# Talking-heads attention with a squared-ReLU feed-forward: reciprocals, copies and tails moved to GpSimd, spread weights made later, and another order of TensorE's units

## The chip, the cores and the metric

The kernel runs on one core of a Trainium2 chip. The metric is the time of one execution on the device in microseconds, as the median of several runs. A lower time is better. Beside the timed runs there is one profiled execution with a hardware trace.

The engines are called by their names or by the short names of the profile: TensorE (PE, and PEld for its weight loads), VectorE (DVE), ScalarE (ACT), GpSimd (POOL) and SyncE (SP). A name with a q behind it (SPq, POOLq) is the engine's queue when it issues a DMA.

## The reference

The inputs are q, k and v of shape (8 batches, 12 heads, 448 positions, 64), two 12 x 12 matrices w_pre and w_post, and the weights of a feed-forward layer, w_in (768 x 2048) and w_out (2048 x 768). All are float32.

```python
scores = scale * np.matmul(q, k.transpose(0, 1, 3, 2))
scores = np.einsum('bhij,hg->bgij', scores, w_pre)      # mixes heads before the softmax
scores = scores - np.max(scores, axis=-1, keepdims=True)
attn = np.exp(scores)
attn = attn / (np.sum(attn, axis=-1, keepdims=True) + 1e-09)
attn = np.einsum('bhij,hg->bgij', attn, w_post)         # mixes heads after it
attn_out = np.matmul(attn, v)
x = attn_out.transpose(0, 2, 1, 3).reshape(B * S, H * D)
h = np.maximum(x @ w_in, 0.0)
out = h * h @ w_out                                     # 3584 x 768, float32
```

## The kernel before, in words

**Pieces of work.** The kernel handles the eight batches one after another, overlapped. For a batch it loads q and k, reorders them by copies from qraw and kraw into qkt (`fn_shf`, "shf", one copy for each of q and k and each of three groups of heads, in batches 1 to 7), transposes them on TensorE, evicts the transposes, and multiplies q by k (`emit_QK`) for tiles of rows. The scores are evicted to `stage` and moved by DMAs on SyncE's queue into `dring`, so that the 12 heads of 10 query rows stand in 120 partitions. Such a set of 10 rows is a chunk, and two chunks are a pair. One matmul group for each pair (`emit_pre`) mixes the heads.

**The softmax.** `after_pre` does the rest for a pair. ScalarE takes the exp out of PSUM into `pring` and sums each row into `sums` (L1215). The reciprocal of the sums goes to `rinv` (`fn_rec`, L1231, VectorE). The division isn't done on the scores but on the weights of the second mixing: `fn_fold` (L1238) multiplies wk2b by `rinv` into `wk2s`, one set of weights for each chunk. The last 64 columns of both chunks use shared weights, so there `fn_tail` (L1249) multiplies the scores themselves by `rinv` into `ptail`. For the first five pairs (`g < 10`) reciprocal, fold and tail are on VectorE. After that the fold is on GpSimd, and the tail goes to VectorE or GpSimd as the planner finds. `emit_post` then mixes the heads with `wk2s` and `ptail`, the result is evicted into `a2t` ("a2ev", L1304), and `emit_AV` multiplies by v. `rinv`, `wk2s`, `pring` and `ptail` are rings of 10 chunks, five pairs: a new pair waits for the users of the pair five before it (`old_users`).

**Feed-forward.** `emit_F1` multiplies by w_in, the ReLU is taken out of PSUM by ScalarE or VectorE (L1458, L1459), VectorE squares (L1468), and `emit_F2` multiplies by w_out. GpSimd issues the output DMAs (L1588), and the loads of q, k, v and the weights.

**The start.** In batch 0 the first chunks go without the moves. VectorE multiplies q by weights (`sc`, L948) and TensorE takes six chunks directly (L1028). Sixteen further chunks take scores from a spread copy of q (L985), and mix heads with `wk1s` (L1006). `wk1s` is made on VectorE (L570) from `wrep3`, which four small DMAs on ScalarE's queue fill (`fn_wspread`, L557). The profile calls this tile wrep too.

**What sets the order.** A planner written in Python (`_Plan`) runs when the kernel is built. Each task has an engine, dependencies, a priority, and for each engine that may do it a pair of times in ns: how long it holds the engine, and when its result is there. TensorE's units are taken from ten streams in the order that the string `ORDER` gives, one character a unit (0 transposes, 1 and c scores, 2, a and b the first mixing in three forms, 3 the second mixing, 4 the multiplication by v, 5 the direct and spread start, 6 to 9 the feed-forward). The other engines take whichever ready task can start earliest, then by priority. A task marked FLEX goes to the engine that would end it first, with `bias` added on VectorE's side. So a changed cost moves nothing by itself but can move tasks between engines and change their order. Each engine then executes its list strictly in the planned order, and semaphores make it wait where the real times are later than the planned. A unit of TensorE that uses the array in another form than the one before it ("quad", "row", "cols", "full") has a change of mode planned at 102 ns. A task marked `two` on VectorE is planned to wait while a `two` task of GpSimd runs.

Of the kernel before, what the change touches and what calls it, by code (L numbers as in the profile page):

```python
# [7 lines left out]
ALU = mybir.AluOpType  # L8
# [20 lines left out]
INF = float("inf")  # L29
STREAM = {"a": 2, "b": 2, "c": 1, **{str(i): i for i in range(10)}}  # L30
ORDER = (
    "00c0010c501551555c55555515555c15555553531c5213a5b5aaa525b030255553aa03250232353c0ab3a03a"
    "c143c244312c673a623bb63762a37763b6ca76173337331c142cb4ba41367673a66727633cc7663227776633"
    "17ac919229393383b002441182383128300240027ac18a3c811c83c3836c3ca67222667733c6631761327722"
    "24442763cc763c36c3761ca002767322276673336621277833811283a8022083003811181318222919133931"
    "39222449c1c933a931393224422443226336c37117c6ca36100a7337321621672237a006336371273422008c"
    "18113811382229392229393181a183338c3c83124222444422363c6c17337a1631603a073c721621673a3736"
    "221673370022442200931933c9c229c8c18a3382218c9c33913a93393114222444228381338c3183c622267a"
    "37c6300c63722176126733373622167220073930019ca393c19c83c182228183c83228a1833c833c4b422244"
    "442236cc63371c76336c62226701077c37362216733722803082218380330913c9c22911922913933c913392"  # L40
    "228c8a3c83383cc4422244442226736373c6cc62276c771c6373621267337812283383382214442293392229"
    "39363368222838338a7367767676733684447667766776677676768798989989899988"
)


# [282 lines left out]
def bass_talking_heads_attention__then__ffn_squared_relu_kernel(  # L328
# [45 lines left out]
    with ExitStack() as es:  # L374
        def sb(name, shape, dtype):
            return es.enter_context(nc.sbuf_tensor(name, list(shape), dtype))
# [34 lines left out]
        nmax = sb("nmax", [128, NPS, 2], DT.float32)  # L411
        test = sb("test", [128, 4], DT.float32)
        flag = sb("flag", [1, 1], DT.int32)
        rinv = sb("rinv", [128, NPS, 1], DT.float32)
        sb("align", [128, 16], DT.uint8)
        w_in_sb = sb("w_in_sb", [128, NFT, FF], DT.bfloat16)
# [42 lines left out]
        def program(safe):  # L459
# [35 lines left out]

            def fn_init(eng, en):
                eng.memset(mask[:, :, :], 1.0)
                eng.memset(wk1r[:, :], 0.0)
                eng.memset(wk1c[:, :, :], 0.0)
                eng.memset(wrep[:, :], 0.0)  # L500
                eng.memset(wk2b[:, :, :], 0.0)
                eng.memset(wk1s[:, :], 0.0)
                eng.memset(wrep3[:, :], 0.0)
                return eng.memset(ident[:, :], 0.0)
# [48 lines left out]
            def fn_wspread(eng, en):  # L553
                for x in range(4):
# [3 lines left out]
                        sem_w3.handle, 16)  # L558
                return None

            t_wspread = plan.add("wspread", ACT, fn_wspread, [t_init], {ACT: (2900.0, 6000.0)},
                                 -1e6, sem_w3, 64)

            def fn_wk1s(eng, en):
# [256 lines left out]
            def emit_T(b):  # L821
                pb = b % 2
                for a in range(3):
                    g = _Group(2)
                    trs = []
                    for i, src in enumerate((qraw, kraw)):
                        o0 = i * S
                        if b == 0:
                            g = _Group(1)
                            o0 = 0  # L830

                        def fn_tr(eng, en, a=a, g=g, i=i, src=src, o0=o0):
                            r_ = None
                            for t in range(0 if b else 2 * NT):
                                o = ((POS[t % NT] if i else t % NT) * 2 + t // NT) * 32
                                for c in range(2):
                                    rows = slice(64 * c, 64 * c + 64)
                                    o_ = ps_bf[rows, g.banks[0], 0:2 * S].rearrange(
                                        "p (u k) -> p u k", u=2)[:, :, o:o + 32]
                                    i_ = src[rows, 2 * a + t // NT, t % NT, :]  # L840
                                    r_ = eng.transpose(o_, i_, ident[rows, rows])
                            for t in range(NT if b else 0):
                                o = o0 + (POS[t] if i else t) * PJ
                                for u in range(2):
                                    rows = slice(64 * u, 64 * u + 64)
                                    i_ = qkt[rows, pb, a, i, :, :].rearrange("p u s -> p (u s)")
                                    r_ = eng.transpose(ps_bf[:, g.banks[u], o:o + PJ],
                                                       i_[:, 2 * D * t:2 * D * (t + 1)],
                                                       ident[rows, rows])
                            return r_  # L850

                        landed = [t_ for t_ in qk_tasks[(b, a)] if t_.name[8:9] == str(i)]
                        if b:
                            def fn_shf(eng, en, a=a, i=i, src=src):
                                return copy(
                                    eng, en,
                                    qkt[:, pb, a, i, :, :].rearrange(
                                        "p u s -> p (u s)").rearrange(
                                        "p (t c d) -> p t c d", c=2, d=D),
                                    src[:, 2 * a:2 * a + 2, :, :].rearrange("p c t d -> p t c d"))  # L860

                            t_shf = add("shf%d_%d_%d" % (b, a, i), FLEX, fn_shf,
                                        landed + [qk_done.get(b - 2)],
                                        {DVE: (400.0, 500.0), POOL: (1500.0, 1620.0)},
                                        b * 1000.0 - 710)
                            t_shf.two = True
                            landed = [t_shf]
                            raw_free[(b, a, i)] = t_shf
                        t_tr = unit(s_T, "tr%d_%d_%d" % (b, a, i), fn_tr, landed + [t_init2],
                                    7 * 32.0 + 20.0 if b else 14 * 32.0 + 33.0,  # L870
                                    "row" if b else "quad", g, 2 * NT if b else 4 * NT)
                        T_of[(b, a, i)] = t_tr
                        raw_free.setdefault((b, a, i), t_tr)
                        trs.append(t_tr)
                        if b:
                            continue
                        for u in range(2):
                            p = 3 * u + a

                            def fn_ev(eng, en, u=u, p=p, g=g, i=i):  # L880
                                return copy(eng, en, qkt[:, 0, p % 3, i, p // 3, :],
                                            ps_bf[:, g.banks[0], u * S:(u + 1) * S])

                            t_ev = add("tev0_%d_%d" % (p, i), FLEX, fn_ev, [t_tr, trev.get((0, p - 3, i))],
                                       {ACT: (447.0, 597.0), DVE: (309.0, 400.0)}, -4e5)
                            g.readers[0].append(t_ev)
                            trev[(0, p, i)] = t_ev
                            if i:
                                trev[(0, p)] = t_ev
                            else:  # L890
                                emit_scale(p)
                                emit_spread(p)
# [252 lines left out]
            def old_users(g):  # L1145
                x = g - g % 2 - NPS
                return [d.get(y) for d in (post_of, fold_of, tail_of) for y in (x, x + 1)]
# [45 lines left out]
            def after_pre(g, t_pre, gr, x):  # L1193
# [34 lines left out]
                p0 = g0 % NPS  # L1228

                def fn_rec(eng, en):  # L1230
                    return eng.reciprocal(rinv[:, p0:p0 + n, :], sums[:, g0:g0 + n, :])  # L1231

                t_rec = add("rec%d_%d" % (b, c), DVE, fn_rec, [exp_of[g0], t_exp] + old_users(g),
                            {DVE: (82.0, 160.0)}, b * 1000.0 - 900 + c)

                def fn_fold(eng, en):
                    i0 = wk2b[:, :, :].rearrange("p a b -> p (a b)").unsqueeze(1)
# [3 lines left out]

                t_fold = add("fold%d_%d" % (b, c), DVE if g < 10 else POOL, fn_fold,
                             [t_rec, t_wk2] + old_users(g),
                             {POOL: (330.0, 370.0), DVE: (200.0, 280.0)},
                             b * 1000.0 - 900 + c)
                t_fold.two = True

                def fn_tail(eng, en):
# [3 lines left out]

                t_tail = add("tail%d_%d" % (b, c), DVE if g < 10 else FLEX, fn_tail,
                             [t_rec, t_exp, exp_of[g0]] + old_users(g),
                             {POOL: (390.0, 430.0), DVE: (210.0, 290.0)},
                             b * 1000.0 - 900 + c)
                t_tail.two = True
                for y in members(g0):
                    fold_of[y] = t_fold
                    tail_of[y] = t_tail  # L1260
# [3 lines left out]
            def emit_post(g0):  # L1264
# [32 lines left out]
                for x in range(n):  # L1297
                    def fn_a2(eng, en, x=x):
# [3 lines left out]
                            "p (o t) -> p o t", t=H5))  # L1302

                    t_a2 = add("a2ev%d_%d" % (g0, x), FLEX, fn_a2, [t_post] + old,  # L1304
                               c_ev(nb * PR), b * 1000.0 - 800 + c0)
                    for g in gs:
                        a2_of[g].append(t_a2)
                    gr.readers[x].append(t_a2)
# [527 lines left out]
```

## Time and profile before

| | |
|---|---|
| median of 3 runs | 539.87 us (537.53 to 541.67) |
| the profiled execution, its time | 539.18 us |
| its span, first to last instruction | 537.4 us |
| mean granted TensorE clock | 0.992 |
| instructions | 22056 |
| bytes moved by DMA | 72.08 MB, mean 134 GB/s |
| DMA issues on GpSimd for outputs, loads of q and k, loads of v | 52, 88, 48 |

The span is shorter than the time by 1.8 us, which lie before the first and after the last instruction. A busy share is the share of the span in which an engine executed. A row of a group names the line, the engine, the operation, the tiles written and read, the shapes and the count. Behind the first bar stand the busy us and the mean ns of one. Behind the second bar stands the idle time just before these instructions and what ended it. In a list of waits the three numbers are total us, times, and longest us. TensorE's busy time counts matmuls from their start to their modelled end, and these overlap, so short gaps between them are not seen.

### The profile page before, as it was taken

The numbers are of one execution on the slowest core, as the hardware profiler recorded it, in microseconds if no ns is written. First come the engines' busy times: TensorE is split into PE (matmuls) and PEld (weight loads), VectorE is DVE, ScalarE is ACT, GpSimd is POOL, SyncE is SP. The second block draws the span as 40 slices with busy tenths as digits, with TensorE's granted clock in tenths as the row PEclk, the third lists the DMA queues.
The fourth block names the chain that finished last, engine by engine and source line by source line (L and its number), as shares of the span: only waits on it lengthen the run. The fifth ranks groups of instructions, "written<-read, shape, count | busy, mean of one in ns | idle before, by whom it ended". The sixth has DMA issues, their size and how long they took to land.

```text
span 537.4 us, 22056 instructions
## 1 busy us (share of the span) xinstructions
PE 512.1 (95%) x8924; PEld 318.9 (59%) x8924; DVE 439.9 (82%) x1187; ACT 454.7 (85%) x1295; POOL 230.9 (43%) x430
## 2 busy tenths in 40 slices
PE   6898999999999999999989998899999999999997
PEld 3345666657765664566546664366645574567964
DVE  6699998899998889978998887987889776977530
ACT  5599999899999899999988897789889998898411
POOL 9513664433572475435653356422923244033000
PEclk9799999999999999999999999999999999999999
DMA  8979999856795589557873589436964566543004
GB/s 175 199 153 156 183 211 182 159 121 133 150 181 124 126 162 166 119 116 153 166 145 73 130 172 180 106 69 141 183 129 98 127 152 131 98 96 73 4 17 107
DMA packets 82519, 72.08 MB, mean 134 GB/s; under 512 B 13502, under 2 KB 79662, under 8 KB 82414
## 3 DMA queue, kind: packets, MB, share of 16 engines
q0 software_dynamic: 36480, 32.58, 38.2%
q1 hardware_dynamic: 45514, 37.83, 29.6%
q8 instruction: 73, 1.20, 0.9%
q10 hardware_dynamic: 420, 0.20, 0.1%
q14 instruction: 32, 0.26, 0.1%
HBM read 45.70 MB, written 11.01 MB: 106 GB/s over the span
## 4 chain that ended last, share of the span: by engine, by line
PE 58%; ACT 20%; DVE 14%; DMA 4%; issue 2%; ACTq 0%; SPq 0%; DVEq 0%
PE ps L1553 23%; PE ps L1425 11%; ACT pring L1215 9%; ACT a2t L486 5%; PE ps L1347 5%; DVE stage L487 4%; PE ps L1285 4%; PE ps L1087 4%; PE ps L1177 4%; ACT stage L486 3%; DVE a2t L487 3%; DMA dring<-stage 2%; PE ps L1399 2%; PE ps L1496 2%; DVE h2t L1468 2%
## 5 line engine op out<-in xcount | busy, mean ns | idle before, releaser
L1215 ACT ACTIVATE pring<-ps 128x448 bf16<-128x448 f32 (+1 forms) x368 | 197.7, 577 | 10.3 <-PE ps L1177 8.0
L1238 POOL TENSOR_TENSOR wk2s<-wk2b,rinv 128x120 bf16<-128x120 bf16 x179 | 76.2, 428 | 192.3 <-DVE rinv L1231 191.7
L1553 PE MATMUL ps<-w_out_sb,h2t 64*128 64x384 bf16 x1664 | 152.0, 323 | 0.3
L1425 PE MATMUL ps<-xt,w_in_sb 64*128 64x448 bf16 (+2 forms) x1344 | 121.8, 322 | 1.4 <-DVE a2t L487 0.8
L486 ACT ACTIVATE a2t<-ps 128x420 bf16<-128x420 f32 x182 | 113.2, 686 | 9.9 <-PE ps L1285 9.2
L487 DVE CAST a2t<-ps 128x420 bf16<-128x420 f32 x178 | 110.6, 648 | 8.8 <-PE ps L1285 7.3
L487 DVE CAST stage<-ps 128x448 bf16<-128x448 f32 (+1 forms) x179 | 107.6, 616 | 11.8 <-PE ps L1087 8.3
L1553 PEld LDWEIGHTS ps<-w_out_sb,h2t 64*128 64x128 bf16 x1664 | 79.0, 94 | 51.4 <-PE ps L1177 2.1
L486 ACT ACTIVATE stage<-ps 128x448 bf16<-128x448 f32 (+1 forms) x181 | 95.0, 568 | 17.1 <-PE ps L1087 16.1
L1215 ACT ACTIVATION_READ_ACCUMULATOR pring<-ps 128x1 f32 (+1 forms) x368 | 89.2, 242 | 0.0
L1425 PEld LDWEIGHTS ps<-xt,w_in_sb 64*128 64x128 bf16 x1344 | 62.1, 94 | 42.0 <-PE ps L1177 2.3
L1588 POOL DMA_DIRECT2D out_dram<-osb x52 | 33.7, 653 | 89.0 <-DVE osb L487 37.5
L1285 PEld LDWEIGHTS ps<-wk2s,pring 60*128 60x128 bf16 x2160 | 52.0, 93 | 30.0 <-issue 3.4
L1285 PE MATMUL ps<-wk2s,pring 60*128 60x60 bf16 x2160 | 60.7, 187 | 4.8 <-DVE rinv L1231 1.5
L1468 DVE TENSOR_TENSOR h2t<-h1t 128x448 bf16<-128x448 bf16 (+2 forms) x176 | 59.6, 367 | 1.4 <-ACT h1t L1458 1.0
L1087 PE MATMUL ps<-qkt 64*128 64x448 bf16 (+1 forms) x360 | 54.1, 356 | 6.6 <-DVE qkt L487 4.2
L1458 ACT ACTIVATE h1t<-ps 128x448 bf16<-128x448 f32 (+2 forms) x98 | 44.1, 470 | 15.4 <-PE ps L1425 13.4
L1249 DVE TENSOR_TENSOR ptail<-pring,rinv 128x128 bf16<-128x128 bf16 x166 | 55.3, 333 | 2.0
L1231 DVE RECIPROCAL rinv<-sums 128x2 f32<-128x2 f32 x184 | 28.9, 157 | 27.2 <-ACT pring L1215 26.6
L1459 DVE TENSOR_SCALAR h1t<-ps 128x448 bf16<-128x448 f32 (+2 forms) x78 | 37.7, 485 | 10.7 <-PE ps L1425 9.6
L1177 PE MATMUL ps<-dring,wk1r 64*64 64x448 bf16 (+1 forms) x550 | 41.1, 362 | 3.4 <-issue 2.1
L1399 PE MATMUL ps<-xt,w_in_sb 128*128 128x220 bf16 (+1 forms) x384 | 42.2, 260 | 0.3 <-ACT a2t L486 0.2
(87 smaller groups left out, 604.9 us busy)
## 6 DMA issues: line engine op xcount, KB each, us to landing
dring<-stage SPq DMA_DIRECT2D x308, 105.0 KB
out_dram<-osb POOLq DMA_DIRECT2D x52, 192.0 KB, 3.9
qraw<-in_q_dram POOLq DMA_DIRECT2D x42, 112.0 KB, 5.3
kraw<-in_k_dram POOLq DMA_DIRECT2D x42, 112.0 KB, 5.0
w_in_sb<-in_moe_w_in_dram POOLq DMA_DIRECT2D x8, 384.0 KB, 8.7
vraw<-in_v_dram POOLq DMA_DIRECT2D x24, 128.0 KB
w_out_sb<-in_moe_w_out_dram POOLq DMA_DIRECT2D x8, 384.0 KB, 11.7
vraw<-in_v_dram POOLq DMA_DIRECT2D x24, 96.0 KB
```

What stands on the lines that cost most here:

```text
L486: return eng.activation(o, i_, AF.Copy)
L487: return eng.tensor_copy(o, i_)
L1087: r_ = eng.matmul(ps[o:o + i_, g.banks[x], 0:S], qkt[r0:r0 + 64, pb, p_ % 3, 0, p_ // 3, i0 + w - i_:i0 + w], qkt[r0:r0 + 64, pb, p_ % 3, ...
L1177: r_ = eng.matmul(ps[64 * y:64 * y + 64, gr.banks[x], 0:S], wk1[64 * x:64 * x + 64 - R0 * x, :], dring[64 * x:64 * x + 64 - R0 * x, (g0 + ...
L1215: return eng.activation(pring[0:r1, pr, 0:S], ps[0:r1, gr.banks[x], 0:S], AF.Exp, accum_out=sums[0:r1, g, :], **bias)
L1238: return eng.tensor_tensor(wk2s[:, p0:p0 + n, :], i0.to_broadcast([128, n, PR]), rinv[:, p0:p0 + n, :].to_broadcast([128, n, PR]), ALU.mult)
L1249: return eng.tensor_tensor(ptail[:, p0 // 2, :, :], pring[:, p0:p0 + n, 0:PJ], rinv[:, p0:p0 + n, :].to_broadcast([128, n, PJ]), ALU.mult)
L1285: r_ = eng.matmul(ps[:, gr.banks[x], o * PR:(o + 1) * PR], p_, w_, start=True, stop=True)
L1399: r_ = eng.matmul(ps[:, g.banks[0], 0:n], w_in_sb[:, ft, t * 128:(t + 1) * 128], xt[:, ft, c0:c1], start=(ft == 0), stop=(ft == NFT - 1))
L1425: r_ = eng.matmul(ps[z * m:(z + 1) * m, g.banks[x], 0:n], w_in_sb[64 * y:64 * y + 64, ft, t:t + m], xt[64 * y:64 * y + 64, ft, c0:c1], sta ...
L1468: return eng.tensor_tensor(h2t[:, t16, o0:o0 + n], h1t[:, s, 0:n], h1t[:, s, 0:n], ALU.mult)
L1553: r_ = eng.matmul(ps[z * m:(z + 1) * m, g.banks[hh], 0:FH], h2t[64 * y:64 * y + 64, t16, col + z * m:col + (z + 1) * m], w_out_sb[64 * y:6 ...
```

## The change

- `fn_rec`: for every pair after the first five the reciprocal is done on GpSimd, as `sums` to the power -1, with a constant tile `minus` as the second operand. One memset for it is added at the start. For the first five pairs it stays on VectorE.
- `fn_shf`: the copy of head pairs may no longer go to VectorE. All are on GpSimd.
- `fn_tail`: VectorE's side gets a bias of 300 ns in the planner's choice, and the costs are changed.
- The fold's cost on GpSimd and the eviction of the second mixing (`a2ev`) get other figures in the planner.
- `t_wspread`: the four small DMAs are planned to hold ScalarE for 3.4 us instead of 2.9, and to have landed 11.6 us after the task's start instead of 6.0. What waits for them is planned later.
- `ORDER` is another string of the same 950 units.

```diff
 ORDER = (
-    "00c0010c501551555c55555515555c15555553531c5213a5b5aaa525b030255553aa03250232353c0ab3a03a"
+    "00c0010c5c05511555555555155555153555522c51225b550c05c1b553325bbb533a5b3a2530a03bb300c3c3"
...
+        minus = sb("minus", [128, 2, 1], DT.float32)
         rinv = sb("rinv", [128, NPS, 1], DT.float32)
...
                 eng.memset(mask[:, :, :], 1.0)
+                eng.memset(minus[:, :, :], -1.0)
...
-            t_wspread = plan.add("wspread", ACT, fn_wspread, [t_init], {ACT: (2900.0, 6000.0)},
+            t_wspread = plan.add("wspread", ACT, fn_wspread, [t_init], {ACT: (3400.0, 11600.0)},
                                  -1e6, sem_w3, 64)
...
-                            t_shf = add("shf%d_%d_%d" % (b, a, i), FLEX, fn_shf,
+                            t_shf = add("shf%d_%d_%d" % (b, a, i), POOL, fn_shf,
                                         landed + [qk_done.get(b - 2)],
-                                        {DVE: (400.0, 500.0), POOL: (1500.0, 1620.0)},
+                                        {POOL: (990.0, 1050.0)},
...
                 def fn_rec(eng, en):
+                    if en == POOL:
+                        return eng.tensor_tensor(rinv[:, p0:p0 + n, :], sums[:, g0:g0 + n, :],
+                                                 minus[:, 0:n, :], ALU.pow)
                     return eng.reciprocal(rinv[:, p0:p0 + n, :], sums[:, g0:g0 + n, :])
 
-                t_rec = add("rec%d_%d" % (b, c), DVE, fn_rec, [exp_of[g0], t_exp] + old_users(g),
-                            {DVE: (82.0, 160.0)}, b * 1000.0 - 900 + c)
+                t_rec = add("rec%d_%d" % (b, c), DVE if g < 10 else POOL, fn_rec,
+                            [exp_of[g0], t_exp] + old_users(g),
+                            {DVE: (82.0, 160.0), POOL: (130.0, 170.0)}, b * 1000.0 - 900 + c)
...
-                             {POOL: (330.0, 370.0), DVE: (200.0, 280.0)},
+                             {POOL: (344.0, 400.0), DVE: (200.0, 280.0)},
...
-                             {POOL: (390.0, 430.0), DVE: (210.0, 290.0)},
+                             {POOL: (350.0, 400.0), DVE: (200.0, 290.0)},
                              b * 1000.0 - 900 + c)
                 t_tail.two = True
+                t_tail.bias = 300.0
...
                     t_a2 = add("a2ev%d_%d" % (g0, x), FLEX, fn_a2, [t_post] + old,
-                               c_ev(nb * PR), b * 1000.0 - 800 + c0)
+                               {ACT: (501.0, 610.0), DVE: (543.0, 632.0)}, b * 1000.0 - 800 + c0)
```

More of the change, by code (lines that the diff above doesn't have):

```diff
@@ L31 @@
 ORDER = (
-    "00c0010c501551555c55555515555c15555553531c5213a5b5aaa525b030255553aa03250232353c0ab3a03a"
[L33 to L42, printed above, removed]
+    "00c0010c5c05511555555555555155553555522c51225b550c05c1b553325bbb533a5b3a2530a03bb300c3c3"
+    "1ac424c4c233a66262772336236b732763b7133763336211444711721aa6662c37733667c323766713a77627"
+    "319c221938293390023812414a8321833430a00270ac8112811c8333811622766231767ca66cc27733336722"
+    "244413267c763c166c37273003176223762267722166738a33812183382200830308ccc811382229c933c933"
+    "19c2244293119ac93339223422444b3a6316337c17136a36100a732c73126126722370063363721272438220"
+    "083318c1181c93a39222939a813c8c3381c381324222444423161a36373137c6a1c6a00733712621673337a6"
+    "12260073372244220093c9ccc93c19228318ca383228c933c933a93c193224442224838113833622816c1733"
+    "722006136a7223763363722176a3367112790000c9c3c91cc92228382238a38a383c381c383cc81324422244"
+    "4422367361c7c6c163700a176333637221762236721178a008333831822290091319a319229339cc39133922"
+    "24418cc833a8c13832244442226716c71631631731733622267a376212673378121833833822244422933933"
+    "922298382238633687a677367633766444877667767686767767676789989999888899"
 )
```

## The prediction

> **What bounds the kernel now.** I read the shares of the page first, then the chain that ended last, then a table of busy time by stage, then the stretches that looked empty.
>
> ```profile
> span 537.4 us, 22056 instructions
> PE 512.1 (95%) x8924; PEld 318.9 (59%) x8924; DVE 439.9 (82%) x1187; ACT 454.7 (85%) x1295; POOL 230.9 (43%) x430
> ...
> PE 58%; ACT 20%; DVE 14%; DMA 4%; issue 2%; ACTq 0%; SPq 0%; DVEq 0%
> ```
>
> TensorE is busy for 95% of the span. Nothing in the change shortens a matmul, so what can be won is what TensorE waits for. That 34% of the chain runs through ScalarE and VectorE says who makes it wait: they empty the eight PSUM banks. The stages (columns: stretch, its length, then busy time of PE, PEld, DVE, ACT and POOL, granted clock, DMA share, GB/s) show where:
>
> ```profile
> 10.00:17.00 7.00, 2.43 (x62) 1.36 (x62) 2.78 (x11) 3.67 (x10) 5.83 (x10) 0.77 1.32 199
> 17.00:25.00 8.00, 8.00 (x60) 3.25 (x58) 5.71 (x19) 4.64 (x11) 3.63 (x5) 0.77 1.33 200
> 25.00:75.00 50.00, 47.69 (x837) 26.96 (x837) 47.37 (x134) 49.87 (x157) 21.39 (x39) 1.00 0.98 174
> 75.00:500.00 425.00, 412.82 (x7405) 258.74 (x7403) 366.17 (x960) 383.94 (x1092) 188.79 (x353) 1.00 0.68 134
> ```
>
> From 10 to 17 us TensorE works 2.43 of 7 us. From 25 to 75 us ScalarE is full and VectorE nearly so. From 75 to 500 us TensorE misses 425 - 412.82 = 12.2 us. The timeline tells what happened at the start:
>
> ```profile
> 11.46 0.63 PE L841 MATMUL ps<-ident,qraw 64*64 64x64 bf16 x28 [0.37 <-DMA qraw<-in_q_dram]
> 14.84 0.35 DVE L570 SCALAR_TENSOR_TENSOR wk1s<-wrep,mask 128x60 bf16<-128x60 f32 x2 [4.19 <-DMA wrep<-in_w_pre_dram]
> 16.12 0.56 PE L1087 MATMUL ps<-qkt 64*128 64x448 bf16 x2 [4.03 <-DVE qkt L487]
> 17.47 0.95 PE L841 MATMUL ps<-ident,kraw 64*64 64x64 bf16 x28
> 22.04 0.36 PE L1087 MATMUL ps<-qkt 64*128 64x448 bf16 x2
> ```
>
> VectorE stood 4.19 us in front of wk1s, an instruction that waits for the spread weights. Behind it in VectorE's queue stood the evictions of the transposes (qkt) that TensorE needed, so TensorE stood 4.03 us. Its clock then fell: the same 28 transposes took 0.63 us before and 0.95 us after.
>
> **The change part by part.** The prices come from the groups by line, shapes apart:
>
> ```profile
> L1231 DVE RECIPROCAL rinv<-sums 128x2 f32<-128x2 f32 x184 | 28.9, 157 | 27.2 <-ACT pring L1215 26.6
> L1249 DVE TENSOR_TENSOR ptail<-pring,rinv 128x128 bf16<-128x128 bf16 x166 | 55.3, 333 | 2.0
> L1249 POOL TENSOR_TENSOR ptail<-pring,rinv 128x128 bf16<-128x128 bf16 x18 | 7.3, 403 | 0.0
> L487 DVE COPY qkt<-kraw 128x896 bf16<-128x896 bf16 x11 | 6.7, 605 | 0.0
> L487 POOL COPY qkt<-qraw 128x896 bf16<-128x896 bf16 x12 | 11.4, 950 | 2.1 <-DMA qraw<-in_q_dram 2.1
> L1238 POOL TENSOR_TENSOR wk2s<-wk2b,rinv 128x120 bf16<-128x120 bf16 x179 | 76.2, 428 | 192.3 <-DVE rinv L1231 191.7
> L517 POOL TENSOR_SCALAR_AFFINE_SELECT mask<-mask 128x10 f32<-128x10 f32 x2 | 0.4, 220 | 0.0
> ```
>
> *Spread weights later.* The planner now expects them 11.6 us after their task starts, which by its own figures (ScalarE free at 1.3 us, initialisation first) is about 1.9 us; so wk1s is due at 13.5 us. VectorE could start it at 14.84, so up to 1.3 us of the wait may stay: the gain is 2.7 to 4.0 us, and I take 3.4. Its only readers, the matmuls of L1006, come after scores that are spread and evicted behind the whole start, so the later place costs nothing. With the stall goes the low clock. From 17 to 25 us TensorE was full at clock 0.77, so at most 8 x 0.23 = 1.8 us, at least nothing if the scaled products of VectorE come last there; I take 0.8. The Trainium skill's page "TensorE: Matmul & The Clock Gate", Part 1, says that an idle window of about 3.4 us puts the clock at half. The trace agrees (4.03 us idle, then 0.95 against 0.63 us); by that rule a rest of 1.3 us would leave the clock whole and the term would be the full 1.8. Start: **-4.2** (-2.7 to -5.8).
>
> *VectorE relieved from 25 to 75 us.* Three tables by stretch, of VectorE's reciprocals, of the tails (VectorE, then GpSimd), and of its copies from qraw and kraw:
>
> ```profile
> 25.00:75.00 50.00, 3.66 (x23) 1.00 0.98 174
> 75.00:500.00 425.00, 25.24 (x161) 1.00 0.68 134
> ...
> 25.00:75.00 50.00, 5.72 (x19) 1.59 (x4) 1.00 0.98 174
> 75.00:500.00 425.00, 49.60 (x147) 5.66 (x14) 1.00 0.68 134
> ...
> 25.00:75.00 50.00, 1.21 (x2) 1.00 0.98 174
> ...
> 25.00:75.00 50.00, 0.61 (x1) 1.00 0.98 174
> ```
>
> The first five pairs keep VectorE for reciprocal and tail. So 18 reciprocals leave (18 x 0.157 = 2.8 us), half of 14 tails (7 x 0.30 = 2.1) and three copies (1.8): 6.7 us. Evictions go to whichever engine is free, so both full engines share it: 3.4 us at most, nothing if the exps alone, which only ScalarE can do, set the pace. TensorE's own idle time there is 2.3 us. I take **-1.7** (0 to -3.4).
>
> *VectorE relieved from 75 to 500 us.* 25.2 us of reciprocals, half of 147 tails (73 x 0.337 = 24.6) and 17 copies (10.3): 60 of 366 us. What TensorE can get of it is what it waited for VectorE there:
>
> ```profile
> PE ps L1285 <- DVE rinv L1231: 1.5, 1, 1.5
> PE ps L1285 <- DVE a2t L487: 1.1, 2, 0.8
> PE ps L1087 <- DVE a2t L487: 0.9, 2, 0.7
> ...
> PE ps L1285 <- DVE stage L487: 0.2, 1, 0.2
> ```
>
> Nine such rows make 5.8 us. The whole is the upper bound, nothing the lower, since a wait that ends on VectorE may next end on ScalarE, which keeps its exps. I take **-2.4**.
>
> *What GpSimd takes on.* 179 reciprocals, about 80 tails, and 20 copies: of 21 copies each from q and k (seven batches, three groups) 21 - 12 = 9 and 11 are on VectorE now. No power on GpSimd is in the trace. Its nearest rows are an operation on 10 floats per partition (220 ns) and the fold on 120 (428 ns); for 2 elements I take 0.22, with the reciprocal's 0.157 and the fold's 0.428 as ends. 179 x 0.22 = 39, 80 x 0.40 = 32, 20 x 0.95 = 19: GpSimd goes from 231 to 321 us, 60% of the span (67% at the upper end). In its fullest stretch (25 to 75 us) 21.4 becomes 21.4 + 4.0 + 2.8 + 2.9 = 31 of 50. The cover is its idle time. The waits of its queue:
>
> ```profile
> POOL wk2s L1238 <- DVE rinv L1231: 191.7, 121, 10.9
> POOL out_dram L1588 <- ACT pring L1215: 29.0, 8, 5.8
> DVE rinv L1231 <- ACT pring L1215: 26.6, 36, 2.3
> POOL qkt L487 <- DMA kraw<-in_k_dram: 5.5, 3, 2.2
> ```
>
> The fold already stood in GpSimd's queue waiting for the reciprocal (191.7 us); now the reciprocal waits there for the exp instead. Behind it stand the fold, tails, loads and output issues; behind twice as many copies, which wait for loads (longest 2.2 us), stand reciprocals. The ring holds five pairs, and a pair passes every 425/161 = 2.6 us, so a fold late by 2 us is covered. VectorE in turn loses the 26.6 us it spent waiting in front of reciprocals, but its remaining tails now wait for GpSimd. I take **0**, between -1.5 (TensorE's own wait for rinv) and what the last rival says. The two engines also hold each other up:
>
> ```profile
> 337.51 1.57 DVE L1249 TENSOR_TENSOR ptail<-pring,rinv 128x128 bf16<-128x128 bf16 x1
> 337.97 0.95 POOL L487 COPY qkt<-qraw 128x896 bf16<-128x896 bf16 x1
> ...
> L1249 DVE TENSOR_TENSOR ptail<-pring,rinv x166: 255/286/1568, 27.8 to 494.3; 128x128 bf16<-128x128 bf16 x166
> ```
>
> A tail of 0.29 us lasted 1.57 while GpSimd copied. Mean less median is 47 ns, 7.8 us in 166 tails. GpSimd's work on data (folds 76, 22 copies of 0.95, tails 7: 104 us) becomes 104 + 39 + 32 + 19 = 194, so 86 tails lose 86 x 47 x 194/104 = 7.5 us, the same again; against 67 us freed this is inside the share taken above. The page "SBUF — State Buffer" of the Trainium skill, section "SBUF: two separate sides", speaks against such a move: port pair locked for whole instructions, the loser fully blocked. The trace agrees (1.57 us); by it the 60 us would be some 52 and the term above -2.1.
>
> *The order.* Reading both strings unit by unit with each unit's mode, TensorE's work is the same; changes of mode go from 261 to 269. One costs:
>
> ```profile
> 83.69 0.54 PE L1087 MATMUL ps<-qkt 64*128 64x448 bf16 x4
> 84.41 1.93 PE L1399 MATMUL ps<-xt,w_in_sb 128*128 128x228 bf16 x18 [0.17 <-ACT a2t L486]
> ...
> 332.01 0.10 PEld L1177 LDWEIGHTS ps<-dring,wk1r 64*64 64x64 bf16 x1 [0.37 <-DVE h1t L1459]
> ```
>
> 0.17 us of matmul idle, 0.37 of weight loading. 8 x 0.17 = **+1.4** (0 to +3.0). The other new figures only steer the planner's choices between engines; I price them at nothing.
>
> *Sum.* -4.2 - 1.7 - 2.4 + 1.4 = -6.9 us. The profiled execution took 539.18 us, so 532.3; the median of the runs is 0.69 above it, so **533.0**. Its own ends are -15.0 (524.9) and +0.3 (540.2).
>
> **The rivals.** (B) *VectorE was the true brake*: each term at its best, 539.87 - 15.0 = 524.9. For it: VectorE and ScalarE on 34% of the chain. Against: TensorE shows 12.2 us to win in 425.
>
> (C) *The start is given back.* The loads keep the DMA engines at shares of 0.98 to 1.33 until 75 us, so a TensorE that comes early may stand before weights; the start and the relief yield nothing lasting but the 1.7 us: 539.87 - 1.7 + 1.4 = 539.6. Against: after 11.5 us no row has TensorE waiting for a load.
>
> (D) *GpSimd's queue becomes the brake, slower.* An output's issue waits there for its eviction (29.0 us in 8 waits, up to 5.8). Reciprocals now stand behind it, and a tail on VectorE that waits for those has no slack: VectorE takes its queue in order (the 4.19 us held up the evictions behind them), so evictions stop too. If half of 29.0 reaches the end: 533.0 + 14.5 = 547.5. It decides once such waits meet VectorE tails, or once a reciprocal costs so much that GpSimd is full. Against: its idle time.
>
> (E) *The tails do not move.* The planner takes GpSimd only where it is free soon enough; if none moves, -4.2 - 1.0 - 1.5 + 1.4 gives 534.6.
>
> **Chances.** Forecast 0.45 (529 to 537), B 0.17, C 0.20, D 0.11, E 0.07. About 1% (5.4 us) is what a measurement of this kernel tells from no change. Faster by more (below 534.5): two thirds of the forecast, B, half of E: 0.50. Within: 0.39. Slower (over 545.3): D, 0.11. The range reaches to just under B and to the near side of D: 523 to 546.
>
> **What would show it.** Right: no wait before wk1s of over 1.5 us, and TensorE's from 10 to 17 us gone; clock near 1 there; VectorE and ScalarE together near 895 - 67 + 8 = 836 us busy; about 179 powers near 0.22 us; 42 copies and about 100 tails on GpSimd; PE busy share up. Wrong: TensorE waiting for w_in_sb or w_out_sb (C), VectorE tails waiting for GpSimd's rinv by tens of us (D), powers of over 0.7 us, or a saving outside the first 75 us larger than the one inside.

## The result and the profile after

The changed kernel takes 582.89 us as the median of 4 runs (581.21 to 586.65), the kernel before on the same chip 538.7 us. The ratio is 1.0823, with a 95% interval of 1.0748 to 1.0897: 44 us slower, where 7 us faster was forecast. The profiled execution took 582.36 us. Every ratio below leaves out slow executions, those over 1.5% above the fastest of the same kernel, so it need not be the quotient of the medians.

The page of the changed kernel (span; busy time by engine; the chain that ended last by engine and by line):

```profile
span 580.6 us, 22040 instructions
PE 525.5 (91%) x8922; PEld 323.0 (56%) x8922; DVE 417.3 (72%) x952; ACT 445.3 (77%) x1255; POOL 403.2 (69%) x706
...
PE 37%; POOL 34%; DVE 14%; ACT 10%; issue 3%; DMA 1%; DVEq 0%; POOLq 0%
PE ps L1560 13%; POOL rinv L1234 13%; PE ps L1432 7%; POOL wk2s L1244 5%; ACT pring L1217 5%; PE ps L1292 3%; DVE a2t L488 3%; POOL out_dram L1595 3%; DVE stage L488 3%; PE ps L1089 3%; POOL ptail L1255 3%; PE ps L1406 3%; POOL vraw L741 2%; POOL kraw L703 2%; PE ps L1354 2%
```

VectorE and ScalarE got lighter, if less than forecast (863 us together, where 836 was said). But a third of the chain now runs through GpSimd, which had no share worth a place before, and its largest line there is the power. The stages (columns as before: length, then PE, PEld, DVE, ACT, POOL, clock, DMA share, GB/s):

```profile
10.00:17.00 7.00, 5.64 (x125) 3.06 (x120) 6.33 (x24) 6.40 (x17) 7.00 (x13) 1.00 1.33 199
17.00:25.00 8.00, 6.87 (x42) 2.82 (x40) 3.55 (x10) 5.07 (x16) 3.48 (x5) 1.00 1.35 197
25.00:75.00 50.00, 43.96 (x781) 25.53 (x783) 41.92 (x100) 42.72 (x130) 37.21 (x66) 0.93 0.96 176
75.00:500.00 425.00, 386.34 (x6664) 235.91 (x6660) 317.58 (x680) 344.71 (x970) 317.12 (x553) 0.98 0.66 126
```

The start is as forecast: TensorE works 5.64 us of the seven, at full clock. From 25 us on every engine but GpSimd is idler than before: TensorE misses 38.7 us of the 425, where it missed 12.2. Its granted clock falls too, to 0.93 and 0.98 in these two stretches, where it was 1.00, and the same matmuls fill 525.5 us of the span instead of 512.1. The groups of the moved work:

```profile
L1234 POOL TENSOR_TENSOR rinv<-sums,minus 128x2 f32<-128x2 f32 x179 | 128.2, 717 | 60.5 <-ACT pring L1217 59.7
L1255 DVE TENSOR_TENSOR ptail<-pring,rinv 128x128 bf16<-128x128 bf16 x89 | 30.6, 344 | 88.9 <-POOL rinv L1234 88.8
L1255 POOL TENSOR_TENSOR ptail<-pring,rinv 128x128 bf16<-128x128 bf16 x95 | 39.2, 413 | 0.0
L488 POOL COPY qkt<-qraw 128x896 bf16<-128x896 bf16 x21 | 20.0, 952 | 5.5 <-DMA qraw<-in_q_dram 5.4
```

The power takes 717 ns for two numbers in each partition; the plan has 130. VectorE's 89 remaining tails waited 88.8 us for it. A stretch of the chain shows how it reaches the end:

```profile
205.90 1.28 POOL out_dram L1595 x2
207.18 0.02 issue
207.20 0.72 POOL rinv L1234
207.92 0.58 POOL qraw L703
...
208.51 0.40 POOL wk2s L1244
208.91 0.67 POOL rinv L1234
209.58 0.62 POOL kraw L703
...
213.55 0.67 POOL rinv L1234
...
214.24 0.04 DVE ptail L1255
...
217.26 2.73 DVE h2t L1475 x2
```

The lines with qraw, kraw, vraw and out_dram are GpSimd's issues of loads and outputs. From 205.90 to 214.24 us GpSimd works almost without a gap (8.28 of 8.34 us), on power, load, fold, power, load, and everything behind it waits. Five powers are 3.6 us of this; five multiplications would be about 1.0 (0.21 us each in the first experiment). Then a tail on VectorE lets the chain pass, and two squares hold it for 2.73 us. The timeline of both engines at that place:

```profile
217.14 3.09 DVE L1475 TENSOR_TENSOR h2t<-h1t 128x448 bf16<-128x448 bf16 x2
...
217.19 0.41 POOL L1244 TENSOR_TENSOR wk2s<-wk2b,rinv 128x120 bf16<-128x120 bf16 x1
...
217.53 0.41 POOL L1255 TENSOR_TENSOR ptail<-pring,rinv 128x128 bf16<-128x128 bf16 x1
217.88 0.93 POOL L488 COPY qkt<-qraw 128x896 bf16<-128x896 bf16 x1
218.75 0.93 POOL L488 COPY qkt<-kraw 128x896 bf16<-128x896 bf16 x1
```

The first of the two squares alone lasted 2.79 us and the second 0.38. The long one overlaps a fold, a tail and two copies on GpSimd and ends just after the last of them, much as a tail was held up before the change.

### The profile page after: what moved, and what is told of

The parts are those of the page before. It is cut to its first block, busy times and chain, and to the rows that moved or that the text cites. A ratio compares the mean times of both kernels' runs of the same rounds, so it can differ in the third digit from the quotient of the medians.

```text
span 580.6 us, 22040 instructions
## 1 busy us (share of the span) xinstructions
PE 525.5 (91%) x8922; PEld 323.0 (56%) x8922; DVE 417.3 (72%) x952; ACT 445.3 (77%) x1255; POOL 403.2 (69%) x706
## 4 chain that ended last, share of the span: by engine, by line
PE 37%; POOL 34%; DVE 14%; ACT 10%; issue 3%; DMA 1%; DVEq 0%; POOLq 0%
PE ps L1560 13%; POOL rinv L1234 13%; PE ps L1432 7%; POOL wk2s L1244 5%; ACT pring L1217 5%; PE ps L1292 3%; DVE a2t L488 3%; POOL out_dram L1595 3%; DVE stage L488 3%; PE ps L1089 3%; POOL ptail L1255 3%; PE ps L1406 3%; POOL vraw L741 2%; POOL kraw L703 2%; PE ps L1354 2%
## 5 line engine op out<-in xcount | busy, mean ns | idle before, releaser
L1234 POOL TENSOR_TENSOR rinv<-sums,minus 128x2 f32<-128x2 f32 x179 | 128.2, 717 | 60.5 <-ACT pring L1217 59.7
L1560 PE MATMUL ps<-w_out_sb,h2t 64*128 64x384 bf16 x1664 | 154.9, 327 | 2.2 <-DVE h2t L1475 1.8
L488 DVE CAST a2t<-ps 128x420 bf16<-128x420 f32 x204 | 124.2, 652 | 12.0 <-PE ps L1292 11.4
L487 ACT ACTIVATE a2t<-ps 128x420 bf16<-128x420 f32 x156 | 96.3, 671 | 35.4 <-PE ps L1292 35.1
L488 DVE CAST stage<-ps 128x448 bf16<-128x448 f32 (+1 forms) x176 | 104.9, 616 | 14.6 <-PE ps L1089 13.0
L1255 DVE TENSOR_TENSOR ptail<-pring,rinv 128x128 bf16<-128x128 bf16 x89 | 30.6, 344 | 88.9 <-POOL rinv L1234 88.8
L1595 POOL DMA_DIRECT2D out_dram<-osb x52 | 34.5, 666 | 81.8 <-ACT pring L1217 31.8
L1217 ACT ACTIVATION_READ_ACCUMULATOR pring<-ps 128x1 f32 (+1 forms) x368 | 83.7, 228 | 0.0
L1475 DVE TENSOR_TENSOR h2t<-h1t 128x448 bf16<-128x448 bf16 (+2 forms) x176 | 63.9, 393 | 0.4
L1466 DVE TENSOR_SCALAR h1t<-ps 128x448 bf16<-128x448 f32 (+2 forms) x96 | 45.9, 485 | 13.7 <-PE ps L1432 11.0
L1465 ACT ACTIVATE h1t<-ps 128x448 bf16<-128x448 f32 (+2 forms) x80 | 35.8, 453 | 23.5 <-PE ps L1432 14.8
```

The source lines that it names most:

```text
L487: return eng.activation(o, i_, AF.Copy)
L488: return eng.tensor_copy(o, i_)
L1217: return eng.activation(pring[0:r1, pr, 0:S], ps[0:r1, gr.banks[x], 0:S], AF.Exp, accum_out=sums[0:r1, g, :], **bias)
L1234: return eng.tensor_tensor(rinv[:, p0:p0 + n, :], sums[:, g0:g0 + n, :], minus[:, 0:n, :], ALU.pow)
L1475: return eng.tensor_tensor(h2t[:, t16, o0:o0 + n], h1t[:, s, 0:n], h1t[:, s, 0:n], ALU.mult)
L1560: r_ = eng.matmul(ps[z * m:(z + 1) * m, g.banks[hh], 0:FH], h2t[64 * y:64 * y + 64, t16, col + z * m:col + (z + 1) * m], w_out_sb[64 * y:6 ...
```

## The experiments

The theory, P: the power costs 0.71 us where the plan has 0.13, and all that stands in order behind it is late. Rivals: M, the move to another engine's queue hurts whatever the price; O, the order or the other parts do.

**The power's price taken away**, `a_rec_mult`:

```diff
-                                                 minus[:, 0:n, :], ALU.pow)
+                                                 minus[:, 0:n, :], ALU.mult)
```

> The changed kernel with one word different: on GpSimd the sums are multiplied by the constant -1 instead of raised to the power -1, so rinv there is not the reciprocal; shapes, queue, plan and order are those of the changed kernel. Theory P (price): the power takes 0.71 us where the plan has 0.13, and everything in order behind it is late; the multiplication should take about 0.2 us and the kernel come to about the blind forecast, 528 to 540 us, with VectorE's wait for GpSimd's rinv down from 88.8 to under 30 us. Rival M (move): any reciprocal on GpSimd couples VectorE's queue to GpSimd's, whatever its price: 560 us or more. Rival O (order and the other parts): 565 us or more, since only the price changes.

531.82 us, ratio 0.9895 (0.9856 to 0.9934). This kernel leaves the reciprocal out and is no replacement; it only prices the operation. P holds, M and O fall: with the same queue, plan and order, one cheaper operation is worth 51 us. Its page, one of its stages, its operation in the list for the tile rinv (minimum, median, maximum in ns), and VectorE's wait for it:

```profile
PE 508.5 (96%) x8922; PEld 316.1 (60%) x8922; DVE 416.6 (79%) x952; ACT 441.7 (83%) x1255; POOL 310.4 (59%) x706
...
PE 68%; DVE 14%; ACT 8%; POOL 5%; issue 2%; DMA 2%; SPq 0%; DVEq 0%; ACTq 0%
...
75.00:500.00 425.00, 414.63 (x7491) 260.26 (x7493) 345.84 (x755) 372.07 (x1052) 254.58 (x589) 1.00 0.68 132
...
L1234 POOL TENSOR_TENSOR rinv<-sums,minus x179: 184/195/431, 33.2 to 486.7; 128x2 f32<-128x2 f32 x179
...
DVE ptail L1255 <- POOL rinv L1234: 34.1, 43, 3.5
```

GpSimd's share of the chain is back to 5%. VectorE's wait for rinv was 34.1 us, a little over the 30 expected. VectorE's busy time is the same in both kernels (416.6 and 417.3 us). TensorE's is 508.5 against 525.5, so 17 of the 51 us are a longer busy time for the same matmuls. The clock in the stretch shown is 1.00 with the multiplication and 0.98 with the power; how much of the 17 us is the clock and how much are matmuls that overlap less was not separated.

**The reciprocal back on VectorE**, `a_rec_dve`: `DVE if g < 10 else POOL` becomes `DVE` for t_rec.

> The changed kernel with the reciprocals of all pairs on VectorE as before; copies, tails, spread weights and the new order stay. Theory P: 530 to 543 us, since the 0.71 us are gone. Rival M: the same. Rival O: 560 us or more, as the order and the moved copies and tails remain.

533.32 us, ratio 0.9903 (0.9859 to 0.9947). So copies, tails, start and order together are worth a gain of 1%.

**The power alone**, `b_pow`: the kernel before with the new `fn_rec` and the new `t_rec`, at the planned 130 ns.

> The kernel before with the reciprocals alone moved to GpSimd as a power, at the planned 130 ns; old order, copies, tails and spread weights. Theory P and rival M: 565 to 590 us, the loss in full, as VectorE's tails (most of them still on VectorE here) wait for a reciprocal of 0.71 us that the plan has as 0.13. Rival O: under 550 us.

580.94 us, ratio 1.0779 (1.0706 to 1.0852). The power by itself, in the old order, makes a loss nearly as large: 42 us, where the whole change makes 44. VectorE's tails, 176 of them here, wait for it:

```profile
DVE ptail L1255 <- POOL rinv L1234: 105.3, 131, 2.7
```

**The planner told the truth**, `a_true_cost`:

```diff
-                            {DVE: (82.0, 160.0), POOL: (130.0, 170.0)}, b * 1000.0 - 900 + c)
+                            {DVE: (82.0, 160.0), POOL: (700.0, 760.0)}, b * 1000.0 - 900 + c)
```

> The changed kernel with the planner told what the power takes: 700 ns held and 760 ns to its result instead of 130 and 170. The work on the chip is the same, the plan around it differs. If the loss is an error of the plan (queues in an order that the real times do not keep), 540 to 560 us and VectorE's wait for rinv under 40 us. If it is the price itself (GpSimd's time, the longer way from exp to the second mixing), 570 to 585 us.

556.57 us, ratio 1.0337 (1.0272 to 1.0401). That is in the first of the two bands. The same operations, 26 us faster: more tails went to VectorE (134 of 184) and its wait for rinv fell:

```profile
DVE ptail L1255 <- POOL rinv L1234: 30.3, 42, 4.1
```

So a little over half of the 51 us is gone once the plan knows the price; the other 25 remain.

**The fourth field**, `a_mult_plan700`: `a_rec_mult` with the plan's 700 and 760 ns.

> The kernel with the multiplication in place of the power (rinv is not the reciprocal), and the planner told 700 ns held and 760 to the result: cheap on the chip, dear in the plan. It fills the fourth field of price by plan. If what hurts is a real time later than the plan, this direction costs little: 530 to 538 us. If any error of the plan costs, 545 us or more.

546.69 us, ratio 1.017 (1.0111 to 1.0229). The expectation that an operation earlier than planned costs nothing was wrong. In medians:

| | plan 130 ns | plan 700 ns |
|---|---|---|
| multiplication, 0.20 us | 531.8 | 546.7 |
| power, 0.71 us | 582.9 | 556.6 |

A plan that is wrong in either direction costs: 15 us when it thinks the operation dear, 26 when it thinks it cheap. With the plan at 700 the price itself is worth only 10 us. So price and plan do not simply add up, and a split of the 51 us depends on which is changed first. The waits of `a_mult_plan700` are of another kind:

```profile
DVE a2t L488 <- PE ps L1292: 28.3, 43, 2.4
...
DVE ptail L1255 <- POOL rinv L1234: 12.6, 12, 3.5
```

VectorE waits less for GpSimd (12.6 us, 34.1 with the plan at 130) and more for TensorE's second mixing (28.3 us, 12.2 with the plan at 130). That the order string, made for the other plan, is to blame was only argued.

**The other string with the true price**, `b_pow_true`: `b_pow` with 700 and 760 ns.

> The kernel before with the reciprocals on GpSimd and the planner told the true 700 and 760 ns; old order, copies, tails and start. If what is left at the true cost (556.6 us in the changed kernel) is a plan that no longer fits its order string, this one, with another string, can come out elsewhere, 545 us or less; if it is the power's price itself, 553 to 568 us (some 4 us more than the changed kernel for the start).

553.39 us, ratio 1.0259 (1.0204 to 1.0314), at the lower edge of the band for the price itself. Against `b_pow` the true figures give back 28 us, as they gave back 26 in the changed kernel. Some 4 us more than `a_true_cost` were expected for the start, and 3 us less came, with intervals that overlap. As the copies, tails and start differ too, this doesn't tell which string fits the true plan better; a string made for it was not tried.

**What the power costs**, `b_price`: the kernel before with twelve operations on constants that nobody reads.

```diff
+            for i, (w, op) in enumerate([(w, op) for w in (2, 2, 4, 16, 64, 128)
+                                         for op in (ALU.mult, ALU.pow)]):
```

> The kernel before with twelve operations of GpSimd added that nobody reads: multiplication and power in turn, float32, 128 partitions by 2, 2, 4, 16, 64 and 128 elements, the base 450 and the exponent -1. Theory P1 (the power has a fixed price): power takes about 0.7 us at 2 elements and little more at 16. Theory P2 (a price for each element): about 0.25 us for each element beyond the 0.2 us of the multiplication, so 1.2 us at 4 and over 4 us at 16. Its time is not compared.

From the timeline of GpSimd; of each size the multiplication comes first, then the power (size 2 twice, the third row is its second multiplication):

```profile
21.23 0.23 POOL L521 TENSOR_TENSOR pout<-pin 128x2 f32<-128x2 f32 x1
21.54 0.73 POOL L521 TENSOR_TENSOR pout<-pin 128x2 f32<-128x2 f32 x1
22.35 0.20 POOL L521 TENSOR_TENSOR pout<-pin 128x2 f32<-128x2 f32 x1
...
23.40 0.24 POOL L521 TENSOR_TENSOR pout<-pin 128x4 f32<-128x4 f32 x1
23.71 1.09 POOL L521 TENSOR_TENSOR pout<-pin 128x4 f32<-128x4 f32 x1
...
25.18 2.90 POOL L521 TENSOR_TENSOR pout<-pin 128x16 f32<-128x16 f32 x1
...
39.31 0.46 POOL L521 TENSOR_TENSOR pout<-pin 128x128 f32<-128x128 f32 x1
39.85 20.78 POOL L521 TENSOR_TENSOR pout<-pin 128x128 f32<-128x128 f32 x1
```

Neither expectation is right as it stands, though the price for each element is nearer. (20.78 - 0.73) / 126 = 0.159 us for each element of a partition, and about 0.4 us fixed: 0.4 + 4 x 0.159 = 1.04 and 0.4 + 16 x 0.159 = 2.94 lie near the rows of 1.09 and 2.90. So the price has a part for each element, and at the two elements of this kernel the fixed part is the larger one. By these rows two pairs at once, four elements, would take 1.09 us against 2 x 0.73 = 1.46; that was not tried in the kernel.

**By which way: VectorE's queue taken out**, `a_tails_pool`: `DVE if g < 10 else FLEX` becomes `DVE if g < 10 else POOL` for t_tail.

> The changed kernel with all tails after the first five pairs on GpSimd, so that no instruction of VectorE waits for the power any more. If the 44 us come through VectorE's queue (its tails waited 88.8 us for GpSimd's rinv, and evictions stood behind them), 540 to 565 us. If they come through GpSimd's own queue (power, fold and tail one after another before the second mixing can start, with loads and outputs between), no gain: 580 to 605 us, as GpSimd takes some 36 us more.

574.49 us, ratio 1.067 (1.0605 to 1.0735), between the two bands. VectorE's wait is gone, and another appears: TensorE itself now waits for a tail that GpSimd ends late.

```profile
PE ps L1292 <- POOL ptail L1255: 22.0, 23, 2.5
...
PE 41%; POOL 37%; ACT 8%; DVE 7%; DMA 4%; issue 2%; POOLq 0%; ACTq 0%
```

**GpSimd's queue shortened by the folds**, `a_fold_dve`: `DVE if g < 10 else POOL` becomes `DVE` for t_fold.

> The changed kernel, power on GpSimd as it is, with all folds on VectorE: GpSimd loses 179 x 0.42 = 75 us, VectorE gets 179 x 0.28 = 50 us and a second instruction in each pair that waits for the power. If GpSimd's queue length makes the 44 us, 545 to 565 us in spite of VectorE's load. If the waiting of VectorE for the power makes them, 585 us or more.

586.12 us, ratio 1.0873 (1.0817 to 1.093): no gain, as the second expectation has it. But the planner then put 170 of 184 tails on GpSimd, so its queue lost only 28 us (403.2 to 374.8), and VectorE's wait went over to the folds, with the same total:

```profile
DVE wk2s L1244 <- POOL rinv L1234: 88.8, 112, 4.1
```

**GpSimd's queue shortened by copies**, `a_pow_oldshf`: the changed kernel with the copies placed by the planner at the old costs.

> The changed kernel with the copies of head pairs where the planner puts them, power on GpSimd as it is. If GpSimd's queue makes the loss, each us taken from it in the stretches of loads comes back: about 20 copies of 0.95 us, so 563 to 576 us. If not, 580 to 586 us.

571.82 us, ratio 1.0614 (1.0562 to 1.0665): 20 us less of work on GpSimd (403.2 to 383.2) gave back 11. The three together fit a loss that goes both ways. Work taken from GpSimd's queue comes back in part; VectorE's wait, taken away, comes back at TensorE. How much of the 44 us goes by which way was not settled, since each removal fed the other.

**The gains, part by part.** `b_wspread`, the kernel before with the later due time alone:

> The kernel before with the later due time of the spread weights alone. Theory S (the start carries the 1% that the changed kernel gains once the power is gone): 533 to 536 us, TensorE's wait of 4.03 us before 16.12 us gone. Rival V (VectorE's relief carries it): 537 to 540 us, as what comes early meets full ScalarE and VectorE until 75 us.

534.44 us, ratio 0.9929 (0.9903 to 0.9954). The stall is gone, and the clock stays whole; wk1s has no wait before it:

```profile
10.00:17.00 7.00, 5.90 (x104) 2.69 (x104) 6.37 (x23) 6.68 (x18) 7.00 (x13) 1.00 1.33 200
...
16.09 0.34 DVE L570 SCALAR_TENSOR_TENSOR wk1s<-wrep,mask 128x60 bf16<-128x60 f32 x2
```

`b_wspread_new`, the kernel of `b_wspread` with the new order:

> The kernel before with the later spread weights and the new order of units; reciprocals, copies and tails as before. If the new order is good by itself, 529 to 533 us; if it only fits the moved copies and tails, 534 to 540 us.

533.96 us, ratio 0.991 (0.9875 to 0.9944), at the edge between the two bands: the new order alone adds nothing that can be told.

`a_rec_dve_old`, as `a_rec_dve` with the old order:

> The changed kernel with reciprocals on VectorE and the old order of units; copies, tails and spread weights as changed. If the new order carries part of the 1%, 535 to 545 us; if not, 531 to 535 us, as with the new order (533.3).

537.32 us, ratio 0.9961 (0.993 to 0.9992), in the first band. The runs spread widely, from 532.26 to 544.03 us, and the interval just overlaps that of `a_rec_dve` (0.9859 to 0.9947). So the new string seems to fit the moved copies and tails better than the old one does, by some 3 us, but this isn't clear of noise.

`a_dve_oldshf`, as `a_rec_dve` with the copies where the planner puts them:

> The changed kernel with reciprocals on VectorE and the copies of head pairs where the planner puts them, as before; tails, spread weights and new order as changed. If the copies on GpSimd help, 535 to 539 us; if they only fill GpSimd's queue, 529 to 533 us (533.3 with them).

530.83 us, ratio 0.9857 (0.981 to 0.9904). It is the fastest kernel that computes the reciprocal, 8 us below the kernel before and 52 below the changed one, though its interval overlaps that of `a_rec_dve`. Its span and the busy times of its engines:

```profile
span 526.3 us, 22046 instructions
PE 508.2 (97%) x8924; PEld 315.9 (60%) x8924; DVE 432.1 (82%) x1131; ACT 448.0 (85%) x1271; POOL 258.3 (49%) x511
```

## Why the prediction was wrong

**The term that failed** is the price of the power: "for 2 elements I take 0.22, with the reciprocal's 0.157 and the fold's 0.428 as ends". It is 0.717, beyond the upper end. The rows used for bounds were of cheap operations: they say what GpSimd needs for an instruction and for moving an element, and nothing of what a power does to an element. Both ends were thus prices of another operation, and an unknown one belongs outside them. With it fell "I take 0" for the waits: 179 x 0.50 = 90 us more in GpSimd's queue, and VectorE's tails waiting 88.8 us where the reciprocals had waited 26.6.

**The plan's own figure** was left out of the sum. The prediction took 0.22 us for an operation that the plan has at 130 ns, and priced nothing for the difference: of the planner's other new figures it says that they "only steer the planner's choices between engines; I price them at nothing". With the power at 0.71 us the true figure in the plan gave back 26 us (`a_true_cost`).

**The cover** claimed for it, "its idle time" and a ring of five pairs, was counted over stretches of 50 and 425 us. With the true price that count would still not have warned: 321 + 90 = 411 of some 533 us is 77%. GpSimd is busy 317 of 425 us after the change, so it is not full on the mean; but where loads, folds and powers meet, it has 8 us almost without a gap. Idle time elsewhere in the stretch did not help there.

**Rival D came true in its place and not in its price.** "GpSimd's queue becomes the brake, slower" at 547.5 was worked out from the outputs' waits of 29.0 us, which hardly changed (31.8). The brake came from the clause added at its end, "once a reciprocal costs so much that GpSimd is full", and from "powers of over 0.7 us", named as what would make the prediction wrong; it had no price of its own, and its chance of 0.11 was too low for an operation that no row showed. The reason given for D, a tail on VectorE waiting in order, holds for the 88.8 us, but `a_tails_pool` shows that the loss finds another way without it.

**The rest of the sum came out right, the relief of VectorE perhaps by luck.** With the power's price away (`a_rec_mult`) the kernel came to 531.8 against the 533.0 forecast. The start was put at -4.2 us; `b_wspread` gives 0.0071 x 538 = 3.8 (2.5 to 5.2). Rival C, the start given back to loads, fell with it. The two relief terms and the order were put at -1.7 - 2.4 + 1.4 = -2.7; from 0.9929 to 0.9895 is 1.8 us, with intervals that overlap, so not told from nothing. And the mechanism of the two relief terms isn't borne out: `a_dve_oldshf` has the reciprocals and half of the copies back on VectorE, which is busy 432.1 us there instead of 416.6, and at 530.83 us it is no slower. So neither these reciprocals nor these copies on VectorE held TensorE up by an amount that shows. What its tails and its order bring beyond the start was not measured apart. The relief was smaller than forecast besides: VectorE and ScalarE together are at 858 us in `a_rec_mult`, not 836. The order, priced at +1.4 alone, showed nothing alone; the gaps of 0.17 and 0.37 us that it was priced by end in their rows on evictions of ScalarE and VectorE, so they did not show the price of a change of mode.

**Tails:** 95 of 184 went to GpSimd, as about 100 were forecast, so E did not come. **The shared hold-up** of the two engines was seen again, with a square of 2.8 us at most, and was not what decided: in `a_rec_mult` GpSimd does the same copies and tails, and VectorE's busy time, which holds the hold-ups, is only 0.7 us less there.

## What to carry to other kernels

An operation that no row shows has no upper bound among the rows of other operations: price it by a run, or leave the range open on that side and give the rival its chance. A kernel whose queues are ordered by a planner pays for a wrong cost twice, once for the operation and once for the order that everything behind it was given: of the 51 us, 26 came back when only the planner's figure was put right. Read the spare time of an engine in the stretch where its work meets, not over the whole span.

## What the runs showed of the hardware

A power on GpSimd (450 to the power -1 in the test) took 0.73 us at 2 float32 elements of a partition, 1.09 at 4, 2.90 at 16 and 20.78 at 128, which is about 0.4 us and 0.159 us more for each element; a multiplication took 0.20 us at 2 elements and 0.46 at 128. A reciprocal of two elements on VectorE took 0.157 us. The power, 0.717 us in the kernel, is thus four to five times as dear as what it replaced, at the smallest size there is here.
